# More identity products on TensorE in an attention and two-MoE kernel

## The chip, the cores and the metric

The kernel runs on one core of a Trainium2 chip. The metric is the device time of one execution in microseconds (us). Engines: PE is TensorE (its weight loads are the queue PEld), DVE is VectorE, ACT is ScalarE, POOL is GpSimd, SP issues the DMAs. L205 is line 205 of the kernel file. The granted clock is given as a share of 2.4 GHz, so 0.50 is 1.2 GHz.

## What is computed

The inputs are q, k, v (4 batches, 8 heads, 576 positions, 64 channels), p (32 positions), and the weights of two MoE layers. All are fp32.

```python
p_packed = sm_attn(p, k, v)             # softmax attention, 32 queries on 576 keys
x = sm_attn(q, p_packed, p_packed)      # 576 queries on 32 keys; heads side by side: (2304, 512)
h = x @ w_in; g = h * cos(h); x = g @ w_out            # first MoE, d_ff 2048
p = domain_probs / (domain_probs.sum(-1, keepdims=True) + 1e-9)
out = sum over e of p[:, e:e+1] * (maximum(x @ w1[e], 0) @ w2[e])   # second MoE, 4 experts, F 1024
```

## The kernel before

Every product of the MoE layers is made of three fp32r products of high and low parts (mm3, L205 to L207). The first phase works by batch: attn_p makes the packed keys, attn_q the attention weights `at`, m_front multiplies the packed values by a block of w_in (the tile wd) to a matrix m, a_front multiplies m and `at` and applies h*cos(h), and a_back multiplies by a block of w_out. The second phase multiplies in seven products per 2x2 block.

The order of the work is not found while it runs. The class Plan takes every piece of work as an op with an engine, a cost in us and a due time (KEYS), and the buffers that it takes; it simulates the engines with these costs and gives each op a start and an end. The program is then issued in the order of these starts (manual_schedule), and each engine works its queue in that order. Semaphores hold what the data and the buffers ask for.

The ops that matter at the start, in TensorE's order: f_s1, f_tr (two), f_pv (two) and f_pp of batch 0, f_s2 of batch 0 (L353), m_front (L353, eight fp32 products; the wd pieces come from POOL, L294), f_s1 of batch 1 (L353), the first two a_fronts (L205 to L207), the two f_tr of batch 1 (L392), a third a_front, f_pv (L409), the fourth a_front, f_pv, f_pp (L432), f_s2 of batch 1 and the next m_front (L353), and then the first a_back.

Between them the other engines work: ACT copies m (L547) and DVE takes its low part (L550); ACT copies `at` (L499) and POOL takes the low part (L658); per a_front ACT rounds (L573), DVE takes the remainder (L576), ACT the sine (L580), DVE multiplies (L583), ACT and POOL split g (L587, L590). ACT's L396 copies the transposes out. ACT, DVE and POOL also split the pieces of w_out (L264 to L297).

PSUM has four buffers for all of this, the tag "pa" of psum2() and psum1(). An op takes one or two and holds them until the last reader is done: an a_front until L583, a transpose until L396.

Identity products: 14 products of the 128x128 identity with itself come at the start (L1254). After the plan is made, the kernel looks at TensorE's ops in their planned order; where the gap before an op is over 1 us of the plan and the op starts before 31, it puts idle(n) into the list at the end of the op before (L1369 to L1372). idle(n) takes a PSUM buffer with psum1() and makes n identity products into it (L1365); nobody reads the result. In the kernel before there is one such gap, with 12 products.

Of the kernel before, what the change touches and what calls it, by code (L numbers as in the profile page):

```python
# [146 lines left out]
def tile_packed_attention_moe_moe2(ctx: ExitStack, tc: tile.TileContext, qT, kT, vk, pT, w_in, w_out, dp, w1, w2, out, out2):  # L147
# [42 lines left out]
    def psum1():  # L190
        return psum2()[:, 0]
# [1170 lines left out]
    def idle(n):  # L1362
        o = psum1()
        for _ in range(n):
            nc.tensor.matmul(o[:, :P], lhsT=ident, rhs=ident, start=True, stop=True)  # L1365

    plan = [(o["start"], o["n"], o["f"]) for o in order]
    plan.append((PROBS, len(plan), probs))
    pe = [o for o in order if o["eng"] == "PE"]  # L1369
    for a, b in zip(pe, pe[1:]):  # L1370
        if b["start"] < 31 and b["start"] - a["end"] > 1:
            plan.append((a["end"], len(plan), lambda n=int((b["start"] - a["end"] - 0.5) / 0.3): idle(n)))  # L1372
    plan.sort(key=lambda x: x[:2])
    ET = mybir.EngineType
    with tc.manual_schedule(engines={ET.PE, ET.Activation, ET.DVE, ET.Pool, ET.SP}):
# [42 lines left out]
```

## Time and profile before

| | us |
|---|---|
| median of 3 runs | 1154.17 |
| lowest, highest | 1151.73, 1157.01 |
| the profiled execution, its own time | 1149.58 |
| its span, first to last instruction | 1147.8 |
| PE busy | 1101.7 (96%) |
| DVE, POOL, ACT busy | 835.3, 633.2, 493.4 |

Busy times are of one execution. The timeline merges instructions of one line that follow each other; an fp32 product of TensorE is two records, an fp32r product or a transpose is one. The brackets behind a row say how long the engine was idle before it and what released it. Ends of matmuls are modelled by the profiler, starts are not.

### The profile page before, as it was taken

The numbers are of one execution on the slowest core, as the hardware profiler recorded it, in microseconds if no ns is written. First come the engines' busy times: TensorE is split into PE (matmuls) and PEld (weight loads), VectorE is DVE, ScalarE is ACT, GpSimd is POOL, SyncE is SP. The second block draws the span as 40 slices with busy tenths as digits, with TensorE's granted clock in tenths as the row PEclk, the third lists the DMA queues.
The fourth block names the chain that finished last, engine by engine and source line by source line (L and its number), as shares of the span: only waits on it lengthen the run. The fifth ranks groups of instructions, "written<-read, shape, count | busy, mean of one in ns | idle before, by whom it ended". The sixth has DMA issues, their size and how long they took to land.

```text
span 1147.8 us, 19120 instructions
## 1 busy us (share of the span) xinstructions
PE 1101.7 (96%) x7241; PEld 1032.5 (90%) x7241; DVE 835.3 (73%) x1244; ACT 493.4 (43%) x852; POOL 633.2 (55%) x477
## 2 busy tenths in 40 slices
PE   6689999999999999999999999999999999999997
PEld 4568999999999988888888889999999999999997
DVE  3798777567555677787777756888887768778776
ACT  3677655445444453244334434333334343333331
POOL 1454755435422775555566546656667767645553
PEclk8699999999999999999999999999999999999999
DMA  9673436433135859787866967676667876666653
GB/s 314 231 263 118 161 116 266 188 130 141 43 105 188 280 196 325 265 301 256 291 257 263 335 259 249 232 252 233 244 227 249 306 265 238 226 227 219 228 182 110
DMA packets 96815, 257.70 MB, mean 225 GB/s; under 512 B 10892, under 2 KB 34516, under 8 KB 94548
## 3 DMA queue, kind: packets, MB, share of 16 engines
q1 hardware_dynamic: 96724, 256.48, 63.1%
q8 instruction: 57, 0.93, 0.3%
q14 instruction: 34, 0.28, 0.1%
HBM read 192.97 MB, written 71.86 MB: 231 GB/s over the span
## 4 chain that ended last, share of the span: by engine, by line
PE 78%; DVE 8%; DMA 5%; issue 4%; ACT 3%; POOL 2%; SPq 0%; POOLq 0%; ACTq 0%; DVEq 0%
PE pa L205 26%; PE pa L207 25%; PE pa L206 25%; DMA w<-w 3%; PE pa L353 2%; DVE pa L958 1%; DVE s L755 1%; POOL aop L658 1%; POOL w L658 1%; DMA kt<-kT 1%; DVE acc L1134 1%; DVE p L958 1%; DVE u L975 0%; DVE oacc L1077 0%; DVE g L1010 0%
## 5 line engine op out<-in xcount | busy, mean ns | idle before, releaser
L205 PE MATMUL pa<-g,w 128*128 128x288 f32 (+1 forms) x960 | 303.6, 316 | 2.0 <-DVE acc L1134 0.8
L206 PE MATMUL pa<-g,w 128*128 128x288 f32 (+1 forms) x960 | 301.6, 314 | 1.2 <-POOL g L590 1.2
L207 PE MATMUL pa<-g,w 128*128 128x288 f32 (+1 forms) x960 | 301.2, 314 | 0.5 <-POOL w L297 0.5
L658 POOL TENSOR_TENSOR g<-u,g 128x384 fp32r<-128x384 f32 x157 | 171.5, 1105 | 140.3 <-ACT g L667 133.5
L205 PE MATMUL pa<-bop,aop 128*128 128x384 f32 x672 | 228.8, 341 | 9.3 <-DVE p L958 4.1
L207 PE MATMUL pa<-bop,aop 128*128 128x384 f32 x672 | 226.9, 338 | 1.5 <-POOL aop L658 1.5
L206 PE MATMUL pa<-bop,aop 128*128 128x384 f32 x672 | 226.3, 337 | 1.1 <-POOL bop L658 1.1
L205 PEld LDWEIGHTS pa<-g,w 128*128 128x128 f32 x960 | 180.1, 188 | 7.9 <-issue 2.4
L206 PEld LDWEIGHTS pa<-g,w 128*128 128x128 f32 x960 | 180.2, 188 | 1.9 <-POOL g L590 1.9
L207 PEld LDWEIGHTS pa<-g,w 128*128 128x128 f32 x960 | 180.4, 188 | 1.0 <-POOL w L297 1.0
L667 ACT ACTIVATE g<-u 128x384 fp32r<-128x384 f32 x192 | 97.2, 523 | 176.8 <-DVE u L987 134.9
L590 POOL TENSOR_TENSOR g<-t,g 128x576 fp32r<-128x576 f32 x64 | 93.2, 1470 | 118.8 <-ACT g L587 117.4
L205 PEld LDWEIGHTS pa<-bop,aop 128*128 128x128 f32 x672 | 126.1, 188 | 19.1 <-DVE p L958 6.1
L206 PEld LDWEIGHTS pa<-bop,aop 128*128 128x128 f32 x672 | 126.2, 188 | 3.0 <-POOL bop L658 1.4
L207 PEld LDWEIGHTS pa<-bop,aop 128*128 128x128 f32 x672 | 126.1, 188 | 2.2 <-POOL aop L658 2.2
L958 DVE TENSOR_TENSOR p<-pa,p 128x384 f32<-128x384 f32 x144 | 79.3, 554 | 41.4 <-PE pa L207 38.7
L1134 DVE TENSOR_TENSOR acc<-pa,acc 128x768 f32<-128x768 f32 x88 | 83.9, 954 | 32.6 <-PE pa L207 31.3
L658 POOL TENSOR_TENSOR w<-w 128x512 fp32r<-128x512 f32 x62 | 86.3, 1403 | 31.4 <-ACT w L705 31.2
L205 PE MATMUL pa<-at,m 128*128 128x288 f32 x256 | 78.7, 307 | 3.1 <-DVE t L583 2.0
L206 PE MATMUL pa<-at,m 128*128 128x288 f32 x256 | 77.5, 303 | 2.8 <-POOL at L658 2.8
L205 PE MATMUL pa<-w,g 128*128 128x512 f32 x192 | 75.9, 395 | 1.9 <-DVE oacc L1077 1.9
L207 PE MATMUL pa<-at,m 128*128 128x288 f32 x256 | 77.2, 301 | 0.0
(129 smaller groups left out, 1924.8 us busy)
## 6 DMA issues: line engine op xcount, KB each, us to landing
at<-at SPq DMA_DIRECT2D x16, 1152.0 KB, 5.3
raw<-w SPq DMA_DIRECT2D x32, 512.0 KB, 5.2
w<-w SPq DMA_DIRECT2D x64, 256.0 KB, 5.0
raw<-w_in SPq DMA_DIRECT2D x6, 1024.0 KB, 6.1
raw<-w_out SPq DMA_DIRECT2D x6, 1024.0 KB, 8.0
vt<-vk SPq DMA_DIRECT2D x8, 576.0 KB, 8.5
kt<-kT SPq DMA_DIRECT2D x8, 576.0 KB, 10.5
qt<-qT SPq DMA_DIRECT2D x8, 576.0 KB, 8.6
```

The costliest lines, as they stand in the source:

```text
L205: nc.tensor.matmul(o, lhsT=l(0), rhs=r(0), start=first, stop=False, skip_group_check=True)
L206: nc.tensor.matmul(o, lhsT=l(0), rhs=r(1), start=False, stop=False, skip_group_check=True)
L207: nc.tensor.matmul(o, lhsT=l(1), rhs=r(0), start=False, stop=last, skip_group_check=True)
L353: nc.tensor.matmul(o(e)[32 * q:32 * q + 32, :N], lhsT=l[64 * e:64 * e + 64, 32 * q:32 * q + 32], rhs=r(q // 2, q % 2)[64 * e:64 * e + 64], ...
L590: nc.gpsimd.tensor_tensor(out=s["g"][:, 1], in0=s["t"], in1=s["g"][:, 0].bitcast(F32), op=ALU.subtract)
L658: (nc.vector if on_vector else nc.gpsimd).tensor_tensor(out=dst[:, 1], in0=src, in1=dst[:, 0].bitcast(F32), op=ALU.subtract)
L667: nc.scalar.activation(r["t"][:, 0], src(), AF.Copy)
L755: nc.vector.tensor_tensor(out=t, in0=src(a, m)(), in1=src(b, m)(), op=o)
L958: nc.vector.tensor_tensor(out=s[o] if o in s else tmp(o), in0=s[x], in1=s[y], op=ALU.add)
L1134: nc.vector.tensor_tensor(out=ac["t"], in0=ac["t"] if how == ALU.subtract else p, in1=p if how == ALU.subtract else ac["t"], op=how)
```

## The change

The condition on the gap now reaches to ops that start before 60 in the plan. For those from 31 on, the number of products is five per us of the gap; below 31 the number is formed as before. The buffers, the plan and the order of all other ops are left as they were.

```diff
     for a, b in zip(pe, pe[1:]):
-        if b["start"] < 31 and b["start"] - a["end"] > 1:
-            plan.append((a["end"], len(plan), lambda n=int((b["start"] - a["end"] - 0.5) / 0.3): idle(n)))
+        gap = b["start"] - a["end"]
+        if b["start"] < 60 and gap > 1:
+            plan.append((a["end"], len(plan), lambda n=int((gap - 0.5) / 0.3 if b["start"] < 31 else 5 * gap): idle(n)))
     plan.sort(key=lambda x: x[:2])
```

## Rows read from the trace of the kernel before

**Rows 1.** The page: busy us, share, instructions; granted clock in 40 slices (tenths).

```profile
PE 1101.7 (96%) x7241; PEld 1032.5 (90%) x7241; DVE 835.3 (73%) x1244; ACT 493.4 (43%) x852; POOL 633.2 (55%) x477
...
PEclk8699999999999999999999999999999999999999
```

**Rows 2.** Stretches: from:to, length, busy us (instructions) by engine, clock, DMA, GB/s.

```profile
1.36:5.79 4.43, 4.43 (x20) 4.43 (x21) 0.00 (x0) 0.00 (x0) 0.00 (x0) 1.00 0.94 252
9.39:12.80 3.41, 2.90 (x32) 0.84 (x32) 0.00 (x0) 0.00 (x0) 0.00 (x0) 0.50 1.02 412
23.04:33.49 10.45, 3.92 (x36) 0.74 (x21) 7.61 (x15) 1.96 (x4) 5.41 (x4) 0.50 0.57 206
33.49:36.69 3.20, 3.20 (x36) 1.58 (x36) 3.15 (x8) 1.23 (x2) 0.00 (x0) 0.50 0.65 204
...
40.10:46.93 6.83, 6.22 (x28) 5.79 (x27) 5.91 (x14) 5.59 (x12) 3.17 (x3) 0.50 1.01 326
46.93:50.34 3.41, 1.44 (x12) 1.21 (x11) 2.29 (x4) 3.13 (x5) 2.82 (x3) 1.00 1.02 404
50.34:53.76 3.42, 3.42 (x51) 3.14 (x53) 0.34 (x3) 2.08 (x4) 2.79 (x2) 0.50 0.89 219
```

**Rows 3.** Timeline of PE around m_front: start, us, engine, line, what, idle before.

```profile
26.20 0.74 PE L353 MATMUL pa<-qt,ptf 64*32 64x288 f32 x2
...
33.49 1.06 PE L353 MATMUL pa<-wd,ptf 64*32 64x512 f32 x2 [5.05 <-POOL wd L294]
...
34.35 1.06 PE L353 MATMUL pa<-wd,ptf 64*32 64x512 f32 x2
```

**Rows 4.** The line of the 12 identity products: ns min/median/max, first and last start.

```profile
L1365 PE MATMUL pa<-ident x24: 275/275/377, 13.0 to 15.7; 128*128 128x128 f32 x24
```

**Rows 5.** Timeline of ACT, POOL and DVE from m_front to L583.

```profile
35.46 1.02 ACT L547 ACTIVATE m<-pa 128x1024 fp32r<-128x1024 f32 x1 [3.33 <-PE pa L353]
...
38.24 2.80 POOL L658 TENSOR_TENSOR at<-xt,at 128x576 fp32r<-128x576 f32 x2 [4.80 <-ACT at L499]
...
40.42 0.89 DVE L271 TENSOR_SCALAR dt<-dt 128x512 f32<-128x512 f32 x1 [1.26 <-ACT dt L264]
...
43.69 1.57 DVE L280 SCALAR_TENSOR_TENSOR dt<-raw,dt 128x512 uint32<-128x512 uint32 x1
...
45.29 0.63 ACT L290 ACTIVATE w<-dt 128x512 fp32r<-128x512 f32 x1 [1.24 <-DVE dt L280]
...
45.83 1.18 ACT L573 ACTIVATE t<-pa 128x576 int32<-128x576 f32 x2
...
49.03 1.42 DVE L583 TENSOR_TENSOR t<-t,pa 128x576 f32<-128x576 f32 x2 [1.12 <-ACT t L580]
```

**Rows 6.** Timeline around the third a_front.

```profile
46.06 1.91 PE L392 MATMUL pa<-ident,a 128*96 128x128 f32 x12
...
49.70 0.75 DVE L583 TENSOR_TENSOR t<-t,pa 128x576 f32<-128x576 f32 x1
...
49.93 0.37 PE L205 MATMUL pa<-at,m 128*128 128x288 f32 x1 [1.97 <-DVE t L583]
...
50.41 0.79 ACT L396 ACTIVATE aT<-pa 96x768 f32<-96x768 f32 x1
...
54.00 0.40 PE L205 MATMUL pa<-at,m 128*128 128x288 f32 x1
...
55.78 0.88 PE L409 MATMUL pa<-vt,aT 96*32 96x64 f32 x48
```

**Rows 7.** Timeline of PE at the end of batch 1's attention.

```profile
58.52 1.20 PE L353 MATMUL pa<-qt,ptf 64*32 64x288 f32 x32 [1.10 <-ACT ptf L436]
59.51 1.07 PE L353 MATMUL pa<-wd,ptf 64*32 64x512 f32 x16
```

**Rows 8.** Stretches after the changed part, as rows 2.

```profile
60.00:80.00 20.00, 18.51 (x268) 14.60 (x253) 19.75 (x43) 13.31 (x18) 11.10 (x8) 1.00 0.73 265
...
100.00:120.00 20.00, 18.53 (x258) 15.12 (x256) 18.10 (x36) 14.99 (x22) 8.61 (x7) 1.00 0.15 61
```

## The prediction

> **What bounds the kernel now.** I read the page first: TensorE is busy 96% of the span, and its slices are full from the third of forty on; only there at the start does the granted clock leave its upper level [rows 1]. So the change, which touches the first 60 us alone, can win only what TensorE loses there, and anything that it adds ahead of the full stretch is passed on to the end. Next I cut the start into stretches by granted clock [rows 2]. The reader is to see a clock that falls and rises: 1.2 GHz (0.50) from 33.49 to 36.69, from 40.10 to 46.93 and from 50.34 to 53.76, 2.4 GHz between and for good afterwards. In those three stretches TensorE works 3.20, 6.22 and 3.42 us. Each rise came after an uninterrupted run of work: some 3.1 us in the stretch from 9.39 (its work begins at 9.75), 3.2 us from 33.49, 3.8 us from 49.93, but 5.8 us from 41.09 on. Then I read what each engine waits for around the gaps [rows 3, 5, 6]: the gap before 33.49 ends with POOL's last piece of wd (5.05 us), and the one before 49.93 with DVE's multiplication L583 (1.97 us). Between the two the chain isn't TensorE's: ACT, DVE and POOL carry it [rows 5].
>
> **How many products, and where.** The planner is plain arithmetic over the costs written at each op. Carried through, its list of TensorE steps has four gaps of over 1 that end between 31 and 60, in its own units: 7.49 between f_s2 of batch 0 and m_front, 4.72 between f_s1 of batch 1 and the first a_front, 4.03 between the two f_tr of batch 1 and the third a_front, and 1.12 between f_pp and f_s2 of batch 1. Five to a unit makes 37, 23, 20 and 5: 85 products. The gap before 31 keeps its 12. All else keeps its order on every engine, and no DMA moves.
>
> **Price of one product.** An fp32 product is two records. At 2.4 GHz 24 records start between 13.0 and 15.7 [rows 4], 0.117 us apart, so 0.235 us, the first of them still slower; I take 0.23. At the lower level 20 to 21 records fill 4.43 us (the row says 1.00, but the records are nearly twice as far apart as at 13 us) [rows 2], 0.42 to 0.44 us; I take 0.43. The plan has reckoned 0.20, less than either.
>
> **Group 1, 37 products.** They come behind f_s2, whose last records start at 26.20 and just after [rows 3], so I start them at 26.7. In the kernel before, six of m_front's eight products ran ahead while POOL finished, and the last two from 33.49 to 35.41 at half clock [rows 3]; now all eight stand behind the group. If the clock rises after 3.8 us, 8.8 products have run, the other 28.2 take 6.5 us, and the group ends at 37.0. m_front at full clock takes 1.07 us [rows 7]: 38.1 instead of 35.41, **2.7 us late**. Bounds: all at full clock, 37 x 0.23 = 8.5, ends 35.2, m_front 36.3, 0.9 late; a rise after 5.8 us, 13.5 products, then 5.4 us, m_front 39.0, 3.6 late. I take 3.8 because it is near three of the four rises.
> Who waits for that: ACT's conversion of m (L547) starts 0.05 us after m_front and stood idle for it 3.33 us [rows 5]; behind it in ACT's queue lie the pieces of w_out and both conversions to `at`, for which POOL waits at 38.24, and ACT's pieces start DVE at 40.42. From there DVE works without a pause to the end of the sign step (43.69 + 1.57), ACT's w follows at 45.29, the roundings t at 45.83, and DVE's product L583 at 49.03 [rows 5]. I find no slack in that chain, so the first L583 ends at 49.78 + 2.7 = 52.5.
>
> **Group 2, 23 products.** f_s1 follows m_front, 1.1 us at full clock (as the 32 records at 58.52 [rows 7]), so the group runs from 39.2 to 44.5. POOL's `at` is ready at 41.04 + 2.7 = 43.7 [rows 5]. The two a_fronts then take twice 1.78 us (12 records from 54.00 to 55.78 [rows 6]), to 48.1. The first is done by 46.3, but ACT only comes to its rounding at 45.83 + 2.7 = 48.5. So group 2 costs **nothing**, with 2.2 us of cover; without the cover it would cost the 0.8 us by which it passes 43.7. The transposes end by 50.0 (at most 1.91 us, as at 46.06 [rows 6]).
>
> **Group 3, 20 products: the term that decides.** Every identity group takes a PSUM buffer, since idle() calls psum1(), and there are four. At this place the two a_fronts hold two until their L583, and the two transposes hold two until ACT's L396. In the kernel before the third a_front waits at just this point for L583, and the first L396 starts only at 50.41 [rows 6]: no buffer is free before 49.78. The gap is a wait for a buffer, so the products can't fill it: they wait themselves, then run between the wait's end and the a_front. TensorE is idle from 50.0 to 52.5, longer than the 1.97 us that came before the fall at 50.34 [rows 2, 6]; so I start them at half clock. 3.8 us give 8.8 products, 11.2 more take 2.6 us: **6.4 us**. Bounds: 4.6 at full clock throughout, 8.6 at half.
> The third a_front starts at 52.5 + 6.4 = 58.9 instead of 49.93, 9.0 late. Queued behind it are the f_pv, the last a_front, f_pp, and on DVE the scaling z and all that follows, which need f_pv.
>
> **What the clock gives back.** That a_front and the first f_pv lasted from 49.93 to 54.00, 4.07 us; at full clock they are as the pair from 54.00 (1.78) and 55.78 (0.88), 2.66 us [rows 6]: **1.4 us back**. The faster first a_fronts and f_s1 give nothing, being behind ACT's chain. The Trainium skill, "TensorE: Matmul & The Clock Gate", section "Why this matters for your kernels", advises against idle gaps between bursts of matmuls, since the clock then falls back; by that alone all 12.84 us of half-clock work would take half, 6.4 us back. The trace agrees that the clock falls in gaps, not that all of the work is on the path; that result is a rival below.
>
> **Group 4, 5 products,** 5 x 0.23 = 1.15 us in a gap of 1.10 that waits for ACT's ptf [rows 7]: 0.05, nothing.
>
> **Sum.** 2.7 + 6.4 - 1.4 = 7.7, less 0.1 for the a_front's former start 0.15 us behind L583: 7.6 at f_s2. From 60 to 80 and from 100 to 120 TensorE still idles 1.49 and 1.47 us [rows 8], at most 3.0 that could take up delay; nearly all waits there are for engines that are late by as much, so I grant 0.6. That leaves **+7.0 us**. The profiled execution took 1149.58 us (span 1147.8), 4.6 below the median 1154.17 of three runs from 1151.73 to 1157.01; it becomes 1156.6, and the median 1161.2.
>
> **Rivals.**
> 1. *Not slower: the clock pays.* If the clock is already up when group 1 starts, it costs 0.9 and group 3 4.6, and if all half-clock work lay on the path, 6.4 would come back: -0.9, 1153.3. It decides from the point at which the groups hold the clock up across the wait at 49 us. For it: three stretches at half. Against: the clock was at half from 23.04 on [rows 2], and ACT's 3.33 us of waiting show who leads. Chance 0.15. By the skill's rule at its best, with groups that cost nothing at all, it is -6.4, 1147.8; against this speaks that 37 products don't fit into 33.49 - 26.7 = 6.8 us at either price. Chance 0.05.
> 2. *Absorbed.* TensorE's later idle time takes the full 3.0 us: +4.6, 1158.8. That the change doesn't do what it says belongs here: with a buffer free in gap 3 the products start at 50.0 at full clock and end at 54.6, 4.7 behind 49.93, and the sum is 4.7 - 1.4 - 0.6 = +2.7. Chance 0.12.
> 3. *Clock down throughout.* Group 1 ends as at its upper bound (3.6) and group 3 takes 8.6: 3.6 + 8.6 - 1.4 - 0.1 - 0.6 = +10.1, 1164.3. For it: the rise that took 5.8 us. Chance 0.13.
>
> **How the numbers follow.** The forecast has 0.55, with its own range +5 to +9 (1159 to 1163). A measurement here tells about 0.5% (5.8 us) from no change: of the 0.55 I put 0.45 above and 0.10 within. Slower: 0.45 + 0.13 = 0.58. Same: 0.10 + 0.12 + 0.15 = 0.37. Faster: 0.05. The range goes from the first form of rival 1 less some scatter, 1152.5, to rival 3 with scatter, 1166.
>
> **What would show it.** Groups of 74, 46, 40 and 10 records with L1366's identity tile. Step 1: m_front ends near 38 and ACT's L547 moves with it. Step 2: the second group ends before ACT's first L573. Step 3: the third group stands behind a wait for DVE L583 and delays the third a_front to about 59. Step 4: f_s2 of batch 1 at about 66 instead of 58.52, and from 120 us on the same rows as before, some 7 us later. The prediction is wrong if the third group runs inside the gap, if L583 doesn't move by the delay of m_front, or if TensorE's idle time between 60 and 120 us shrinks by more than 1 us.

## The result and the profile after

The medians of eight runs each are 1159.89 us after and 1151.88 us before, 8.0 us more; the ratio is 1.0067 with a 95% interval of [1.0047, 1.0088]. The change made the kernel slower. The profiled execution took 1160.48 us (span 1158.7). Four single runs far outside the rest (one of before with 1216 us, one each of no_g3, g3_spare and g3_double with 1524 to 2780 us) count in no ratio below.

On the page of after, TensorE is busier by 15.7 us and by 170 instructions, the two records of each of 85 products; in the clock row the first two slices go from 8 and 6 [rows 1] to 9 and 8, the rest is as it was:

```profile
PE 1117.4 (96%) x7411; PEld 1050.8 (91%) x7411; DVE 831.4 (72%) x1244; ACT 492.5 (43%) x852; POOL 634.4 (55%) x477
...
PEclk9899999999999999999999999999999999999999
```

The timeline of TensorE in after (start and duration in us, engine, line, operation, count, and the idle time before with its releaser), single records of the a_fronts left out. It answers to [rows 3, 6, 7]:

```profile
26.30 0.68 PE L353 MATMUL pa<-qt,ptf 64*32 64x288 f32 x4 [1.95 <-issue]
26.90 10.16 PE L1365 MATMUL pa<-ident 128*128 128x128 f32 x74
36.99 1.09 PE L353 MATMUL pa<-wd,ptf 64*32 64x512 f32 x16
...
38.98 5.40 PE L1365 MATMUL pa<-ident 128*128 128x128 f32 x46
44.13 0.38 PE L205 MATMUL pa<-at,m 128*128 128x288 f32 x1
...
47.41 1.47 PE L392 MATMUL pa<-ident,a 128*96 128x128 f32 x12
52.76 7.25 PE L1365 MATMUL pa<-ident 128*128 128x128 f32 x40 [3.88 <-DVE t L583]
59.77 0.38 PE L205 MATMUL pa<-at,m 128*128 128x288 f32 x1
...
61.53 0.88 PE L409 MATMUL pa<-vt,aT 96*32 96x64 f32 x48
62.34 0.40 PE L205 MATMUL pa<-at,m 128*128 128x288 f32 x1
...
65.43 0.33 PE L432 MATMUL pa<-ident,pz 128*128 128x128 f32 x1 [0.44 <-DVE pz L416]
65.59 1.28 PE L1365 MATMUL pa<-ident 128*128 128x128 f32 x10
66.85 1.28 PE L353 MATMUL pa<-qt,ptf 64*32 64x288 f32 x32
```

The reader is to see the four groups of L1365, of 74, 46, 40 and 10 records. Three of them follow the work before at once. The third has a bracket: it waited 3.88 us for DVE's L583, and only then ran its 7.0 us, with the third a_front behind it.

The timeline of ACT and DVE in after, which answers to [rows 5]:

```profile
38.18 1.02 ACT L547 ACTIVATE m<-pa 128x1024 fp32r<-128x1024 f32 x1 [5.99 <-PE pa L353]
...
48.66 1.17 ACT L573 ACTIVATE t<-pa 128x576 int32<-128x576 f32 x2
...
53.24 0.79 ACT L396 ACTIVATE aT<-pa 96x768 f32<-96x768 f32 x1
...
51.86 1.42 DVE L583 TENSOR_TENSOR t<-t,pa 128x576 f32<-128x576 f32 x2 [1.12 <-ACT t L580]
...
62.48 0.28 DVE L416 TENSOR_SCALAR pz<-pa,rs 128x64 f32<-128x64 f32 x1 [8.94 <-PE pa L409]
```

ACT's L547 is 2.72 us later than before and DVE's L583 2.83 us. DVE then stands idle for 8.94 us, until f_pv has run behind the third group.

The stretches of after by granted clock, and two later ones; columns as in [rows 2, 8]:

```profile
27.39:30.81 3.42, 3.42 (x18) 3.42 (x18) 3.42 (x9) 0.25 (x1) 1.26 (x1) 0.50 0.76 284
30.81:51.29 20.48, 18.07 (x186) 16.49 (x185) 15.40 (x31) 12.93 (x23) 7.87 (x6) 1.00 0.76 256
51.29:58.11 6.82, 5.35 (x25) 5.38 (x26) 1.65 (x4) 3.06 (x5) 4.05 (x4) 0.50 0.63 155
58.11:75.00 16.89, 15.23 (x224) 12.68 (x224) 11.59 (x23) 10.97 (x15) 7.94 (x6) 1.00 0.49 148
...
60.00:80.00 20.00, 18.16 (x266) 14.53 (x264) 16.52 (x33) 15.31 (x22) 8.93 (x7) 1.00 0.66 221
...
100.00:120.00 20.00, 18.16 (x269) 14.70 (x269) 15.93 (x31) 12.81 (x17) 9.08 (x8) 1.00 0.06 24
```

From 30.81 to 51.29 the clock stays up, as the products were to bring about. It falls at 51.29, in TensorE's wait, and most of the third group runs at half clock.

**Where the time went.** The third a_front is 9.84 us later than in [rows 6]: 2.83 from L583, 7.01 from the third group. From there to the fourth a_front it takes 2.57 us instead of 4.07, which gives 1.50 back. 2.83 + 7.01 - 1.50 = 8.34, and f_s2 of batch 1 starts 8.33 later than in [rows 7]. Nothing of it comes back. The same row of DVE in before and in after, from the timeline of each:

```profile
111.82 0.75 DVE L481 TENSOR_REDUCE z<-x 128x18 f32<-128x576 f32 x1 [0.26 <-ACT x L477]
```

```profile
120.15 0.75 DVE L481 TENSOR_REDUCE z<-x 128x18 f32<-128x576 f32 x1 [0.26 <-ACT x L477]
```

And the first starts of L958, in the rows of that line in before and in after:

```profile
L958 DVE TENSOR_TENSOR p<-pa,p x144: 537/557/560, 400.3 to 1126.6; 128x384 f32<-128x384 f32 x144
```

```profile
L958 DVE TENSOR_TENSOR p<-pa,p x144: 539/557/560, 408.6 to 1137.5; 128x384 f32<-128x384 f32 x144
```

The distance is 8.33 us at 112 us and 8.3 at 400, and by the medians of the same DVE instructions over stretches of 40 us it stays within 0.2 of that up to some 600 us. Behind that it wanders between 7.2 and 10.9, and it ends at 10.9. These two executions lie 2.30 below and 0.59 above their medians, together 2.9, which is about what the end adds; that the wander is chance and not the change isn't shown by one profile of each.

### The profile page after: what moved, and what is told of

Same layout as the page of the kernel before. It is cut to its first block, busy times and chain, and to the rows that moved or that the text cites. A ratio compares the mean times of both kernels' runs of the same rounds, so it can differ in the third digit from the quotient of the medians.

```text
span 1158.7 us, 19461 instructions
## 1 busy us (share of the span) xinstructions
PE 1117.4 (96%) x7411; PEld 1050.8 (91%) x7411; DVE 831.4 (72%) x1244; ACT 492.5 (43%) x852; POOL 634.4 (55%) x477
## 4 chain that ended last, share of the span: by engine, by line
PE 79%; DVE 7%; DMA 6%; issue 3%; POOL 2%; ACT 2%; SPq 1%; POOLq 0%; ACTq 0%; DVEq 0%
PE pa L205 25%; PE pa L207 25%; PE pa L206 24%; DMA w<-w 3%; PE pa L1365 2%; PE pa L353 2%; DVE pa L958 1%; DVE s L755 1%; POOL aop L658 1%; POOL w L658 1%; DMA w<-q7w 1%; DMA kt<-kT 1%; DMA w<-q0w 1%; DVE p L958 1%; DVE acc L1134 0%
## 5 line engine op out<-in xcount | busy, mean ns | idle before, releaser
L958 DVE TENSOR_TENSOR p<-pa,p 128x384 f32<-128x384 f32 x144 | 79.3, 554 | 41.2 <-PE pa L207 38.4
L205 PE MATMUL pa<-at,m 128*128 128x288 f32 x256 | 77.3, 302 | 0.0
L206 PE MATMUL pa<-at,m 128*128 128x288 f32 x256 | 75.7, 296 | 1.1 <-POOL at L658 1.1
L958 DVE TENSOR_TENSOR pa<-pa,p 128x384 f32<-128x384 f32 x96 | 54.1, 563 | 31.0 <-PE pa L207 28.8
```

What stands on the lines that cost most here:

```text
L205: nc.tensor.matmul(o, lhsT=l(0), rhs=r(0), start=first, stop=False, skip_group_check=True)
L206: nc.tensor.matmul(o, lhsT=l(0), rhs=r(1), start=False, stop=False, skip_group_check=True)
L958: nc.vector.tensor_tensor(out=s[o] if o in s else tmp(o), in0=s[x], in1=s[y], op=ALU.add)
```

## The experiments

All kernels here are the changed kernel with other numbers of products in the four groups, and two of them with another target for the third group (below); the counts of after are (37, 23, 20, 5). Their edit is this, with its own COUNTS for each:

```diff
-    def idle(n):
+    def idle(n, g=0):
...
+    COUNTS = (37, 23, 0, 5)
+    group = 0
...
-            plan.append((a["end"], len(plan), lambda n=int((gap - 0.5) / 0.3 if b["start"] < 31 else 5 * gap): idle(n)))
+            n = int((gap - 0.5) / 0.3)
+            if b["start"] >= 31:
+                n, group = COUNTS[group], group + 1
+            if n:
+                plan.append((a["end"], len(plan), lambda n=n, g=group: idle(n, g)))
```

The theory: group 3 has no PSUM buffer before L583, so it runs between L583 and the a_front that waits for L583, and its whole length lies on the path. The rivals: group 1 alone delays everything; or the products cost what they take of TensorE, wherever they stand; or the clock decides. Times are the ratio to before, with its 95% interval, times before's median of the same chip.

| kernel | counts | ratio | us | f_s2 of batch 1, against 58.52 before |
|---|---|---|---|---|
| after | 37, 23, 20, 5 | 1.0067 [1.0047, 1.0088] | +7.7 | +8.3 |
| no_g3 | 37, 23, 0, 5 | 1.0019 [1.0002, 1.0037] | +2.2 | +4.6 |
| only_g3 | 0, 0, 20, 0 | 1.0023 [1.0003, 1.0044] | +2.6 | +4.0 |
| g3_spare | 37, 23, 20, 5, other target | 1.0007 [0.9989, 1.0025] | +0.8 | +1.1 |
| fit | 19, 19, 17, 5, other target | 0.9976 [0.9958, 0.9994] | -2.8 | -1.8 |
| only_g1 | 37, 0, 0, 0 | 1.0012 [0.9997, 1.0027] | +1.4 | +3.1 |
| only_g2 | 0, 23, 0, 0 | 0.9997 [0.9979, 1.0014] | -0.3 | -1.2 |
| only_g4 | 0, 0, 0, 5 | 1.0005 [0.9987, 1.0023] | +0.6 | -1.3 |
| g3_double | 37, 23, 40, 5 | 1.0084 [1.0055, 1.0113] | +9.7 | +13.3 |

The last column is from one profile each, and where the clock falls differs from run to run (below), so it carries an error of one to two us that the ratio does not.

**Without group 3.** COUNTS = (37, 23, 0, 5).

> As the changed kernel, but without the third group (20 products); groups of 37, 23 and 5 stay. Theory (the third group stands behind a wait for a PSUM buffer, so its whole length is added): the third a_front starts at about 52.6 (with L583) and f_s2 of batch 1 at about 61.3; the whole is 2.7 us slower than the kernel before, about 5 faster than the changed one. Rival A (the delay comes from m_front, 2.7 us late, and grows along ACT's and DVE's queues): about 8 slower than before, as the changed kernel. Rival B (the clock pays, the third group alone spoils it): faster than before by 1 to 3 us.

It took 2.2 us more than before. Its timeline of TensorE and the stretch around the third a_front:

```profile
37.98 1.09 PE L353 MATMUL pa<-wd,ptf 64*32 64x512 f32 x16
...
53.71 0.58 PE L205 MATMUL pa<-at,m 128*128 128x288 f32 x1 [3.84 <-DVE t L583]
...
63.09 1.28 PE L353 MATMUL pa<-qt,ptf 64*32 64x288 f32 x32
```

```profile
52.10:58.93 6.83, 5.22 (x62) 4.81 (x63) 2.14 (x6) 4.29 (x7) 4.19 (x4) 0.50 0.68 161
```

The wait for L583 is as long as in after, 3.84 us, but now the a_front itself stands behind it. Taking group 3 out is worth 5.5 us of after's 7.7. The trace lies 1.8 us behind the expectation (f_s2 at 63.09, not 61.3): m_front ends 1.0 us later than in after, and L583 with it; and the clock fell at 52.10, so the third a_front and f_pv ran at half clock to their end (4.58 us up to the fourth a_front, against 4.07 in before).

**Group 3 alone.** COUNTS = (0, 0, 20, 0).

> The kernel before with the third group (20 products) alone. Theory (wait for a buffer, then 20 products): the group starts at 49.8, when L583 is done, lasts 6 to 7 us at mostly half clock, the third a_front starts at about 56.5 and f_s2 of batch 1 at about 63.7; 5 us slower than before. Rival A (m_front's delay is the cause): no slower than before by over 1 us. Rival B (products fill the gap of 1.97 us): 2 to 3 us slower.

It took 2.6 us more than before (0.3 to 5.1), about half of what was expected. As a number that is what rival B has; the trace has to decide. Its timeline of TensorE and its stretches:

```profile
50.94 4.70 PE L1365 MATMUL pa<-ident 128*128 128x128 f32 x40 [2.82 <-DVE t L583]
...
62.50 1.21 PE L353 MATMUL pa<-qt,ptf 64*32 64x288 f32 x32 [1.09 <-ACT ptf L436]
```

```profile
25.69:46.17 20.48, 12.20 (x73) 7.24 (x73) 16.90 (x34) 9.99 (x18) 8.28 (x7) 0.50 0.73 245
46.17:70.00 23.83, 18.18 (x249) 15.07 (x248) 14.79 (x31) 16.52 (x24) 14.44 (x11) 1.00 0.65 200
```

Here too the group waits for L583, with nothing added ahead of it: the wait for a buffer isn't due to group 1 or 2, and rival B, by which the products fill the gap, falls. But the clock had been at half until 46.17 and stayed up after that, so the 20 products took 4.5 us, as in the lower bound of the prediction (4.6), and the a_front and f_pv behind them ran at full clock too. 4.5 less 1.5 is 3.0, close to the 2.6 measured; the 4.0 of f_s2 hold 1.0 more, as this profile's L583 is 1.0 late (50.04) with nothing added ahead of it.

**The same products in columns that nobody needs.** If the wait for a buffer is the cause, products that need no buffer of their own must cost next to nothing. The second transpose's tile has 1024 columns; the transposes write the first 768, and L396 reads no others. Group 3 writes into the last 128.

```diff
             def f_tr(e=e):
                 s["tpv", e] = tpv = psum2().rearrange("p c n -> p (c n)")
+                if bb == 1:
+                    spare[e] = tpv
...
-    def idle(n):
-        o = psum1()
+    def idle(n, g=0):
+        o = spare[1][:, 896:1024] if g == 3 else psum1()
```

> As the changed kernel, all four groups, but the third group writes into columns 896 to 1023 of the second f_tr's own PSUM tile, which nobody reads, so it takes no buffer of its own. Theory (the buffer is what it waits for): the group starts right behind the transposes, near 49.0 in place of 52.8, runs at full clock, ends at 53.5, 0.9 behind L583; the third a_front at about 53.5 at full clock, f_s2 of batch 1 at about 60.7; 2 to 3 us slower than before, 5 to 6 faster than the changed kernel. Rival (the length of the group costs, wherever it waits): as the changed kernel, about 8 slower than before.

It took 0.8 us more than before, which can't be told from nothing. Its timeline of TensorE, its row of DVE's L583 (L586 here, as lines are two or three higher) and its stretches:

```profile
48.08 4.63 PE L1368 MATMUL pa<-ident 128*128 128x128 f32 x40
...
52.46 0.38 PE L205 MATMUL pa<-at,m 128*128 128x288 f32 x1
...
59.57 1.28 PE L353 MATMUL pa<-qt,ptf 64*32 64x288 f32 x32
```

```profile
51.21 1.42 DVE L586 TENSOR_TENSOR t<-t,pa 128x576 f32<-128x576 f32 x2 [1.12 <-ACT t L583]
```

```profile
22.61:29.43 6.82, 6.11 (x45) 3.73 (x46) 4.35 (x10) 1.03 (x2) 3.44 (x3) 0.50 0.89 316
29.43:70.00 40.57, 38.93 (x480) 34.25 (x479) 31.86 (x62) 29.43 (x45) 20.60 (x16) 1.00 0.72 237
```

The group has no bracket: it starts at 48.08, behind the transposes, and runs inside the wait; the clock stays up from 29.43 on. The 85 products are all still there, so it isn't their number that costs, but where one group of 20 stands. Buffer and clock are undone here together: by the trace the two are worth 7.0 - 0.5, as the first of the two products L583 ends at 51.95 and the group ends 0.5 us past it. A further 0.65 us of the gain is not that of group 3: L583 itself comes that much earlier than in after (51.21 against 51.86), because group 1 starts 0.4 us earlier here and has 0.5 us less of half clock. That is part of why f_s2 comes at 59.57 and not at the expected 60.7.

**Groups that fit their gaps.** The target as above and the counts cut to what the gaps of the trace hold.

> Groups of 19, 19, 17 and 5 products, cut so that each ends before what TensorE waits for there (POOL's last wd piece at 33.4, POOL's at, L583), the third one in the spare columns of the second f_tr's tile. Theory (products that fit cost nothing, and the clock gives back only what lies on the path): m_front ends 1.4 us earlier at full clock, L583 with it, the third a_front and f_pv last 1.4 us less; f_s2 of batch 1 at about 55.7, 2.9 us faster than before. Rival (the products cost what they last): slower than before. Rival (all half-clock work is given back): 6 us faster.

It took 2.8 us less than before, and its interval excludes no change: the one kernel of this study that is shown to be faster than before. Its timeline of TensorE:

```profile
27.41 5.48 PE L1368 MATMUL pa<-ident 128*128 128x128 f32 x38
...
34.05 0.62 PE L353 MATMUL pa<-wd,ptf 64*32 64x512 f32 x2 [0.16 <-POOL wd L294]
...
44.88 3.96 PE L1368 MATMUL pa<-ident 128*128 128x128 f32 x34
49.69 0.37 PE L205 MATMUL pa<-at,m 128*128 128x288 f32 x1 [0.85 <-DVE t L586]
...
56.77 1.28 PE L353 MATMUL pa<-qt,ptf 64*32 64x288 f32 x32
```

Behind the first and the third group the old wait is still there, 0.16 us for POOL and 0.85 us for DVE, so neither is late; and all that runs from 29.47 on runs at full clock. The third a_front starts 0.24 us earlier than before, and the 1.5 us between it and the fourth are saved: f_s2 is 1.75 earlier. It was expected 2.9 earlier, at about 55.7: POOL's last piece of wd starts 0.55 us later in this profile than in before (32.70 against 32.15), so m_front ends only 0.3 us earlier (35.10 against 35.41) and not 1.4. The times have 2.8, with 0.7 to 4.8 in their interval, so trace and times don't contradict each other; one trace doesn't show the whole 2.8.

**Each of the others alone.** COUNTS = (37, 0, 0, 0), (0, 23, 0, 0) and (0, 0, 0, 5).

> The kernel before with the first group (37 products) alone. Theory (m_front is late by the part of the group that passes POOL's last wd piece, and ACT's and DVE's queues hand that on to L583): m_front ends 2 to 3 us later, the first L583 with it, the whole is 2 to 3 us slower. Rival (the chain behind m_front has slack, or the clock that the group lifts pays it back): within 1 us of before.

> The kernel before with the second group (23 products) alone. Theory (it ends about 1.5 us behind POOL's at, but the two a_fronts then run at full clock and ACT's queue comes to its rounding no earlier than before): L583 where it was, within 1 us of before. Rival (its length counts): 4 to 5 us slower. Rival (the half-clock work of the a_fronts, 3 us, is given back): 2 to 3 us faster.

> The kernel before with the fourth group (5 products) alone, ahead of f_s2 of batch 1. Theory (1.1 us of products in a wait of 1.1 us for ACT's ptf): within 0.5 us in the trace at f_s2, no difference in time. It also shifts the turn of the four PSUM buffers for all that follows. Rival (that turn costs something in the rest of the kernel): slower by 2 us or more, growing after 60 us.

Group 1 alone took 1.4 us more, less than the 2 to 3 that were expected and just above its rival's 1. Its timeline of TensorE:

```profile
37.38 1.09 PE L353 MATMUL pa<-wd,ptf 64*32 64x512 f32 x16
...
53.03 0.37 PE L205 MATMUL pa<-at,m 128*128 128x288 f32 x1 [3.16 <-DVE t L583]
```

m_front ends at 38.47, 3.06 us later than before, and the a_front is 3.1 later: no slack in the chain between. The trace has twice the loss that the times have, and the interval (-0.3 to +3.1 us) just takes it in; it takes in no loss at all, too. That group 1 moves L583 is shown, by this trace and that of after; what it costs in time is not.

Groups 2 and 4 alone are not to be told from before. The timeline of group 4's kernel:

```profile
50.12 0.37 PE L205 MATMUL pa<-at,m 128*128 128x288 f32 x1 [2.49 <-DVE t L583]
...
55.79 0.33 PE L432 MATMUL pa<-ident,pz 128*128 128x128 f32 x1 [0.43 <-DVE pz L416]
55.95 1.28 PE L1365 MATMUL pa<-ident 128*128 128x128 f32 x10
57.22 1.28 PE L353 MATMUL pa<-qt,ptf 64*32 64x288 f32 x32
```

From f_pp to f_s2 it is 1.43 us, as in before (57.09 to 58.52), so its products cost nothing. Yet f_s2 is 1.3 us earlier than before, though nothing is changed ahead of 55 us: the clock didn't fall at 50 in this run. Group 2's kernel shows the same 1.2, and its time shows no gain, so it isn't put down to group 2.

**Group 3 doubled.** COUNTS = (37, 23, 40, 5).

> The changed kernel with 40 products in the third group in place of 20. Theory (each product behind the wait for L583 is added in full): the group starts where it did in the changed kernel (52.8), the 20 further products take 0.22 to 0.24 us each, 4.4 to 4.8 us more; 12 to 13 us slower than the kernel before. Rival (the wait and the clock cost, not the length): as the changed kernel, about 8 slower than before.

```profile
53.13 11.79 PE L1365 MATMUL pa<-ident 128*128 128x128 f32 x80 [3.88 <-DVE t L583]
...
71.77 1.27 PE L353 MATMUL pa<-qt,ptf 64*32 64x288 f32 x32
```

The group is 4.54 us longer, 0.227 for each of the 20 more, and f_s2 is 4.92 later than in after: by the trace every further product lies on the path at its full-clock price. The times are less clear. The ratio gives +9.7 us (6.3 to 13.0, from three runs) where 12 to 13 were expected; the median of the three, 1162.57, lies 11.7 above before's 1150.88, where after's lies 8.0 above its own.

**How the parts add.** The four alone give 1.4 - 0.3 + 2.6 + 0.6 = 4.3 us, all of them together 7.7. The intervals of the five figures together leave some 5 us of error on the difference of 3.4, so the times alone don't show that there is one. The traces show one: the clock under group 3, which took 4.5 us at full clock when alone and 7.0 in after, 2.5 more. Why the clock is up at that place in one kernel and down in the other isn't settled: in after, no_g3 and g3_double, whose wait for L583 is 3.8 to 3.9 us long, it fell; in only_g3 and only_g4, with 2.8 and 2.5 us, it stayed up; but in before it fell with 1.97 us [rows 2, 6]. So the length of the wait alone doesn't decide.

## Why the prediction was right, step by step

The sign, the deciding term and the size were right: +7.0 us was predicted, +8.0 measured.

- **Group 1** went as put: clock up 3.91 us after the group's start (3.8 assumed), its end at 37.0, m_front's end at 38.08 (38.1). L583 moved by 2.83 us (2.7). That the size fits so well is in part luck: the clock was still up for the group's first 0.5 us (it fell at 27.39, where the prediction had it at half from the start), and in the five other kernels with a first group it rose between 2.1 us (fit) and 4.6 us (g3_double) after that group's start.
- **Group 2** cost nothing, as put. The group ended 0.4 us after the 43.7 at which `at` was to be ready, with ACT's rounding only at 48.66 (48.5).
- **Group 3** is the mis-sized term: 7.0 us, not 6.4, inside the bounds of 4.6 and 8.6. The reason was right, shown by g3_spare: no buffer, so the group stands behind L583. What failed is the choice of the rise after 3.8 us: the clock rose 5.35 us after the group's start, nearer to the one rise at 5.8 that the prediction had seen and set aside. In only_g3 and g3_spare the same 20 products ran at full clock from their start, so the term could have come out at the lower bound as well; the rows of before could not tell which.
- **The clock's gift** was 1.5 us (1.4). The 0.1 for the a_front's former start behind L583 didn't come: that 0.15 us now stands ahead of the group.
- **Group 4** cost nothing, as put.
- **Absorption**, granted 0.6, was 0: f_s2 is 8.33 later and so is DVE's L481 at 112 us. TensorE's idle time in the two later stretches didn't shrink (1.84 us each, against 1.49 and 1.47 in [rows 8]).

Together 0.13 + 0.6 - 0.1 + 0.1 + 0.6 = 1.3, from 7.0 to 8.3 at f_s2.

The absolute time is off by as much the other way, 1159.9 against the 1161.2 predicted: the base of 1154.17 was the median of three runs and over eight it is 1151.88, 2.3 lower, which outweighs the 1.0 by which the change was put too small.

Of the rivals, "the clock pays" has something in it, but not in this form: by fit's trace the clock is worth 1.5 us at this place and 1.75 at f_s2, by its times 2.8 (0.7 to 4.8), if the third group takes no buffer and the groups end before what the engine waits for. "Absorbed" and "clock down throughout" fall. That the clock falls in gaps, as the prediction read it, is loosely put: the falls at 23.04, 40.10 and 50.34 in before came 0.4 to 0.5 us after TensorE had resumed from a wait; that at 51.29 in after came within one.

## What to carry to other kernels

Before filling an idle gap, ask what the gap waits for: a filler that needs the same buffer waits for the same event and is added behind it, at full length. Give it a target that is already held, and make it so short that the old wait is still seen behind it in the trace, with room to spare: the same group lasted 4.4 to 7.0 us here, by the clock that it met. Its count is to come from the traced gap and the traced price of one filler, not from a plan's units.

## What the runs showed of the hardware

- **The price of an identity product.** 128x128x128 in fp32 is two records and takes 0.227 us back to back at full clock (4.54 us for 20), and at half clock about 0.43 us: from the third group's start in after, 52.76, to the rise at 58.11, 25 records in 5.35 us.
- **The clock's falls move between runs.** In before it fell at 50.34; in only_g4, whose program is the same up to 55 us, it was down from 32.44 to 46.09 and then stayed up:

```profile
32.44:46.09 13.65, 10.40 (x60) 7.50 (x61) 12.28 (x26) 9.25 (x18) 5.23 (x4) 0.50 0.86 290
46.09:70.00 23.91, 19.57 (x276) 15.73 (x275) 19.24 (x40) 20.54 (x30) 15.12 (x12) 1.00 0.83 274
```

  One profile can so be 1.3 us off at f_s2 with nothing changed. A gain of that size in a trace is to be believed only with the times beside it.
- **Starts out of program order.** In before, products of m_front start ahead of f_s2's last ones, which stand earlier in the program (the later two are in [rows 3], at 26.20). Both are products of 64 rows, and in the kernel they go to the two halves of the array's rows by turns; that the ones ahead used the other half is not shown:

```profile
25.89 1.08 PE L353 MATMUL pa<-wd,ptf 64*32 64x512 f32 x4
```
